# A static order planned in twelve passes forwards and backwards, and two squares moved to GpSimd, in a kernel of masked attention and a gated feed-forward network

## The chip, the cores and the metric

The kernel runs on one core of a Trainium2 chip. The metric is the device time of one execution in microseconds (us). PE is TensorE (the matrix unit), ACT is ScalarE, DVE is VectorE, POOL is GpSimd, and SP issues most DMAs.

## The reference

Attention over 8 batches, 8 heads, 576 positions and 64 channels: the first four heads see a local window of 32 positions, the other four every 32nd position. Its output is the input of a gated network of 4608 tokens with 512 channels and 1536 hidden ones. All is in 32-bit floats.

```python
scores = scale * np.matmul(q, k.transpose(0, 1, 3, 2))
mask_local = (rel >= 0) & (rel < stride)
mask_strided = (rel >= 0) & (pos[None, :] % stride == pos[:, None] % stride)
...
attn = attn / (np.sum(attn, axis=-1, keepdims=True) + 1e-09)
attn_out = np.matmul(attn, v)
...
rms = np.sqrt(np.mean(x * x, axis=-1, keepdims=True) + 1e-06)
xn = x / rms * rms_g
g = xn @ w_gate
silu = g * (1.0 / (1.0 + np.exp(-g)))
val = xn @ w_val
return (silu * val @ w_out).astype(np.float32)
```

## The kernel before

**Products.** The tokens are cut into 9 chunks of 512 and the hidden channels into 12 units of 128. A unit of a chunk is a `g` product, a `v` product and an `o` product, each in four groups of three matmuls of 128x512: both operands are split into a high and a low part, and the three matmuls are high by high, high by low and low by high (`xh`, `xl` for the input, `hh`, `hl` for the hidden values, `w` or `z` for the weights). `g` and `v` have one PSUM bank each. ACT takes the tanh of `g` (L835), DVE forms the gate from it and from `g` (L837, which frees the bank `g`) and multiplies by `v` (L849, which frees the bank `v`), ACT rounds the result to `hh` (L856), GpSimd forms the rest `hl` (L864), and one unit later the `o` product adds into four accumulators (L877). At the end of a chunk ACT or DVE copies each accumulator out (L884).

**Attention.** It comes in 96 units (batch, pair of heads, third of the rows), 12 for each batch of 576 tokens, a little ahead of the products that need them. Fifteen units run first; the others lie between the product groups. A unit is: scores on PE (L537, or L548 and L552 for the first 27), mask and maximum on DVE (L575, L577, L578), exp on ACT (L590), reciprocal of the sum on DVE (L595, L596), normalisation on GpSimd (L599), 32x32 transposes on DVE (L641; PE and ACT for the early units), the product with the values on PE (L678) and its evacuation to `raw` (L713). For each pair of heads after the 27th unit ACT rounds q and k (L444) and DVE subtracts to get their rests (L449). `raw` is squared and summed for the norm (L724 for chunk 0; L737, L742 and the matmul L747 later), scaled (L774, L778) and split into `xh` (L791) and `xl` (L806).

**Weights.** In the first 150 us each of 36 weight tiles is loaded and unpacked: L950, L957 and L970 on ACT, L961 and L963 on DVE, and a subtraction, L974, on GpSimd or DVE.

**What sets the order.** Nothing is emitted where it stands in the source. `op` records each step with its cost on each engine that could do it, and what it reads and writes. `Plan.order` then gives each step a due time, the length of the longest chain of costs from it to the end with its sign turned, and builds the schedule once, forwards: of the steps that can start, each engine takes the one that is due first, and of several engines the one that ends first. Steps marked `port` on DVE, and all of GpSimd, are never planned at the same time. The order of that schedule is the order in which each engine executes.

Of the kernel before, what the change touches and what calls it, by code (L numbers as in the profile page):

```python
# [94 lines left out]
NPB = 2  # L95
NTB = 3
SPU = 9
GRE = 'DVE'
RCE = 'ACT'
PP0 = 27  # L100
# [30 lines left out]
class Plan:  # L131
# [8 lines left out]
    def __init__(self):  # L140
        self.ops = []
        self.writer = {}
        self.readers = {}
        self.serial = False
        self.last_pe = None

# [24 lines left out]
        self.ops.append((ways, deps, bytes_, rel, lock, tab, chain))  # L171

    def order(self):
        ops, n = self.ops, len(self.ops)
        left = [len(o[1]) for o in ops]
        users = [[] for _ in range(n)]
        for i, o in enumerate(ops):
            for d in o[1]:
# [3 lines left out]
        for i in range(n - 1, -1, -1):  # L182
            ways, _, nb, _, _, _, chain = ops[i]
            eng = min(ways, key=lambda e: ways[e][0])
            own = ways[eng][0] + (DMT if nb else self.TAIL[eng])
            t = max([-due[u] + (0.0 if eng in ops[u][0] else self.LAT) for u in users[i]], default=0.0) + own
            if chain:
                t = chained = max(t, chained + ways[eng][0] * CHF)
            due[i] = -t
        end, on = [0.0] * n, [None] * n  # L190
        ready = [None] * n
        free, avail = {}, {}
# [27 lines left out]
        while len(out) < n:  # L220
            best = None
            for e, lst in avail.items():
                cand = []
                for i in lst:
                    s = start(i, e)
                    ways = ops[i][0]
                    if len(ways) > 1:
                        f = s + ways[e][0] - MARG
                        if any(x != e and start(i, x) + ways[x][0] < f for x in ways):
                            continue  # L230
                    cand.append((s, due[i], i))
# [12 lines left out]
            done = s + cost + self.TAIL[e]  # L244
            for b in lock:
                held[b] = (done, e)
            if pt:
                port = (done, e)
            for x in ways:
                avail[x].remove(i)  # L250
            free[e] = s + cost
            on[i] = e
            if nb:
                dma = max(dma, s) + nb / 380.0
                end[i] = dma + 2000.0
            else:
                end[i] = done
            out.append(fn)
            for u in users[i]:
                left[u] -= 1  # L260
                if not left[u]:
                    enter(u)
# [4 lines left out]
def attn_moe(ctx: ExitStack, tc: tile.TileContext, qT: bass.AP, kT: bass.AP, vl: bass.AP, vs: bass.AP,  # L267
# [151 lines left out]
    def split(o, at):  # L419
        first = 3 * o == FP  # L420

        def part(fn, src, key, more=()):
            ways = [("ACT", act(S), False), ("DVE", 375, True)] if not more else [("DVE", dve(S), True), ("Pool", pool(S), True)]
            if "g" not in ALT:
                ways = ways[:1]
            op(*ways[0][:2], at, fn, reads=[("xx", src)] + list(more), writes=[key], port=ways[0][2], also=ways[1:])
# [187 lines left out]
    def step_t(i):  # L614
# [35 lines left out]
        def trans():  # L650
# [1 line left out]
                nc.tensor.transpose(out=pp[:, x // nt, x % nt * m:(x % nt + 1) * m], in_=pv[:, x // nt, x % nt], identity=ident[:m, :m])  # L652
        op("PE", (PF if i < n_pro else 1) * 2 * nt * 0.85 * m + 30, at + PE_T, trans, reads=[pk, "ident"], writes=[TK, ("S", pn)] if i >= FP - 3 else [TK],
           lock=locks)
        op("ACT", act(2 * nt * m, True), at + 1500, lambda e: nc.scalar.copy(out=dv, in_=pp) if e == "ACT" else
           nc.vector.tensor_copy(out=dv, in_=pp), reads=[TK], writes=[tk], lock=locks, also=way("d", ("DVE", dve(2 * nt * m), False)))

    def step_o(units):

# [60 lines left out]
    def square(c, p, at):  # L720
        rt = raw[c % 2]
        dst, dk = (ssq, "ssq") if p % 2 == 0 else (srt, "srt")
        if c == 0:
            op("ACT", act(CH), at, lambda: nc.scalar.activation(out=dst, in_=rt[:, p], func=AF.Square),  # L724
               reads=[("raw", 0, p)], writes=[dk])

            def sums():
                for t in range(4):
# [53 lines left out]
    def convert(c, at, kcs=range(KC)):  # L782
        rt = raw[c % 2]
        for kc in kcs:
# [14 lines left out]
            def lo(e, kc=kc):  # L799
# [5 lines left out]
                else:  # L805
                    (nc.vector if e == "DVE" else nc.gpsimd).tensor_tensor(out=o, in0=i, in1=h, op=ALU.subtract)  # L806
            r = [("raw", c % 2, kc), "gt"]
            op("ACT", act(CH), at + kc, hi, reads=r, writes=[("xh", kc)] + [("spare", kc)] * (c == 0),
               also=way("j", ("DVE", 345, True)))
            op("DVE", dve(CH), at + kc, lo, reads=r + [("xh", kc)], writes=[("xl", kc)] + [("spare", 4 + kc)] * (c == 0), port=True,  # L810
               also=[("Pool", pool(CH), True)] if c else [])

# [122 lines left out]
    for x, key in enumerate(keys):  # L935
# [11 lines left out]
        def scale(e, hi32=hi32):  # L947
# [2 lines left out]
                nc.scalar.activation(out=h, in_=h, func=AF.Copy, scale=2.0 ** -112)  # L950
            else:
                nc.vector.tensor_scalar(out=h, in0=h, scalar1=2.0 ** -112, scalar2=None, op0=ALU.mult)
        op("ACT", 561, at, scale, writes=[("w", key)], rel=CV0 + CVP * x, also=way("a", ("DVE", 345, True)))

        def last3(e, lo32=lo32, top=top):
            if e == "ACT":
# [10 lines left out]
        def hi(e, key=key, z=z):  # L967
# [5 lines left out]
        op("ACT", act(512), at, hi, reads=[zk], writes=[("w", key), "worder"], also=way("c", ("DVE", 345, True)))  # L973
# [143 lines left out]
```

## Time and profile before

| | us |
|---|---|
| median of 3 runs | 1062.4 (1061.9 to 1063.38) |
| profiled execution | 1061.61 |
| its span, first to last instruction | 1059.8 |
| PE busy | 1028.4 |
| DVE busy | 704.6 |
| ACT busy | 545.1 |
| GpSimd busy | 284.5 |

A busy time counts stretches in which at least one instruction of the engine is under way. Matmuls are pipelined, so PE's stalls show best in the distance from one start to the next.

### The profile page before, as it was taken

How to read it: one execution, taken by the hardware profiler on the slowest of the kernel's cores; microseconds unless marked ns; L12 is line 12 of the kernel's file. 1: busy time of each engine (PE TensorE's matmuls, PEld its weight loads, DVE VectorE, ACT ScalarE, POOL GpSimd, SP SyncE). 2: the span in 40 equal slices, each digit the busy share in tenths (PEclk: the TensorE clock that was granted, in tenths of full speed). 3: DMA queues.
4: the chain of work that ended last, by engine and by line, in shares of the span. 5: the costliest groups of instructions: out<-in, count | busy, mean ns of one | idle time of the engine just before them, and what ended most of it. 6: DMA issues, size and time to landing. Idle time of an engine off the chain costs nothing.

```text
span 1059.8 us, 14841 instructions
## 1 busy us (share of the span) xinstructions
PE 1028.4 (97%) x5212; PEld 825.7 (78%) x5212; DVE 704.6 (66%) x1508; ACT 545.1 (51%) x1459; POOL 284.5 (27%) x263
## 2 busy tenths in 40 slices
PE   7989999999999999999999999999999999999998
PEld 5767667787788778887788788887888888878886
DVE  6899997688857877688757975888578631232111
ACT  6988855556455555555636554564545441132112
POOL 5213433232212321233122222222122322111111
PEclk9899999999999999999999999999999999999999
DMA  9854120211111111011111201111110010001001
GB/s 321 276 195 167 37 68 16 74 36 52 35 63 35 41 47 63 17 53 38 44 47 35 61 16 62 36 49 39 62 34 15 1 40 1 1 0 41 1 1 40
DMA packets 26715, 59.86 MB, mean 56 GB/s; under 512 B 2896, under 2 KB 7184, under 8 KB 26640
## 3 DMA queue, kind: packets, MB, share of 16 engines
q1 hardware_dynamic: 26320, 58.32, 16.9%
q8 instruction: 41, 0.67, 0.3%
q10 hardware_dynamic: 320, 0.59, 0.2%
q14 instruction: 34, 0.28, 0.1%
HBM read 49.46 MB, written 9.44 MB: 56 GB/s over the span
## 4 chain that ended last, share of the span: by engine, by line
PE 74%; DVE 13%; ACT 8%; issue 2%; DMA 2%; POOL 0%; ACTq 0%; POOLq 0%; SPq 0%; DVEq 0%
PE v L822 23%; PE g L822 23%; PE acc L877 21%; ACT qk L444 3%; PE pair L678 3%; DVE qk L449 2%; PE pair L537 2%; DVE pT L641 2%; DMA w<-in_wgv_dram 2%; DVE z L963 1%; DVE e L849 1%; ACT pp L590 1%; DVE w L961 1%; DVE e L837 1%; DVE w L974 1%
## 5 line engine op out<-in xcount | busy, mean ns | idle before, releaser
L864 POOL TENSOR_TENSOR hl<-e,hh 128x512 fp32r<-128x512 f32 x107 | 141.6, 1324 | 383.7 <-ACT hh L856 340.9
L822 PE MATMUL g<-xh,w 128*128 128x512 f32 x648 | 205.3, 398 | 5.9 <-DVE e L837 5.9
L822 PE MATMUL v<-xh,w 128*128 128x512 f32 x648 | 204.1, 396 | 1.7 <-DVE e L849 1.6
L837 DVE SCALAR_TENSOR_TENSOR e<-e,g 128x512 f32<-128x512 f32 x108 | 73.7, 683 | 192.0 <-ACT e L835 190.8
L877 PE MATMUL acc<-w,hh 128*128 128x512 f32 x648 | 200.8, 391 | 0.0
L599 POOL TENSOR_TENSOR pp<-pp,su 96x512 f32<-96x512 f32 (+3 forms) x87 | 85.7, 985 | 313.9 <-DVE su L596 256.7
L590 ACT ACTIVATE pp<-pp,mx 96x128 f32<-96x128 f32 (+2 forms) x296 | 114.0, 386 | 101.0 <-DVE mx L578 91.4
L641 DVE STREAM_TRANSPOSE pT<-pp 32x128 f32<-32x128 f32 (+1 forms) x489 | 141.5, 289 | 30.3 <-POOL pp L599 18.6
L835 ACT ACTIVATE e<-g 128x512 f32<-128x512 f32 x108 | 64.0, 593 | 161.4 <-PE g L822 148.1
L822 PEld LDWEIGHTS v<-xh,w 128*128 128x128 f32 x648 | 119.7, 189 | 29.4 <-DVE e L849 4.9
L822 PEld LDWEIGHTS g<-xh,w 128*128 128x128 f32 x648 | 116.8, 189 | 31.8 <-DVE e L837 8.5
L877 PEld LDWEIGHTS acc<-w,hh 128*128 128x128 f32 x648 | 121.0, 188 | 25.9 <-issue 0.2
L822 PE MATMUL g<-xl,w 128*128 128x512 f32 x324 | 127.0, 392 | 0.0
L822 PE MATMUL v<-xl,w 128*128 128x512 f32 x324 | 127.0, 392 | 0.0
L877 PE MATMUL acc<-w,hl 128*128 128x512 f32 x324 | 126.1, 389 | 0.0
L856 ACT CAST hh<-e 128x512 fp32r<-128x512 f32 x107 | 66.3, 620 | 112.4 <-PE acc L877 90.9
L444 ACT CAST qk<-xx 64x576 fp32r<-64x576 f32 x138 | 88.7, 671 | 8.7 <-PE pair L537 6.4
L849 DVE SCALAR_TENSOR_TENSOR e<-e,v 128x512 f32<-128x512 f32 x108 | 73.5, 681 | 16.2 <-PE v L822 10.4
L449 DVE TENSOR_TENSOR qk<-xx,qk 64x576 fp32r<-64x576 f32 x92 | 72.4, 787 | 2.9
L822 PEld LDWEIGHTS v<-xl,w 128*128 128x128 f32 x324 | 61.2, 189 | 13.4
L822 PEld LDWEIGHTS g<-xl,w 128*128 128x128 f32 x324 | 61.1, 189 | 13.2
L877 PEld LDWEIGHTS acc<-w,hl 128*128 128x128 f32 x324 | 60.8, 188 | 12.8
(166 smaller groups left out, 1490.9 us busy)
## 6 DMA issues: line engine op xcount, KB each, us to landing
w<-in_wgv_dram SPq DMA_DIRECT2D x18, 512.0 KB, 6.5
xx<-in_qT_dram SPq DMA_DIRECT2D x27, 288.0 KB, 2.9
xx<-in_kT_dram SPq DMA_DIRECT2D x25, 288.0 KB, 3.1
vt<-in_vl_dram SPq DMA_DIRECT2D x16, 384.0 KB, 5.3
vt<-in_vs_dram SPq DMA_DIRECT2D x16, 315.0 KB
w<-in_wo_dram SPq DMA_DIRECT2D x9, 512.0 KB, 6.4
out_dram<-ssq SPq DMA_DIRECT2D x17, 256.0 KB, 2.1
out_dram<-srt SPq DMA_DIRECT2D x17, 256.0 KB, 2.0
```

The source lines that it names most:

```text
L444: nc.scalar.copy(out=d, in_=s)
L449: (nc.gpsimd if eng == "Pool" else nc.vector).tensor_tensor(out=d, in0=s, in1=y.bitcast(F32), op=ALU.subtract)
L590: nc.scalar.activation(out=pv[:, h, x], in_=sp[h][:, x] if i < PM else pv[:, h, x], func=AF.Exp, scale=0.125 if i < PM else 1.0, bias=mx[: ...
L599: (nc.vector if e == "DVE" else nc.gpsimd).tensor_tensor(out=pv, in0=pv, in1=su.unsqueeze(3).broadcast_to([m, 2, nt, n]), op=ALU.mult)
L641: nc.vector.transpose(out=dst[32 * y:32 * y + 32, :, 32 * x:32 * x + 32], in_=src[32 * x:32 * x + 32, :, 32 * y:32 * y + 32])
L822: nc.tensor.matmul(out=bank[bk], lhsT=wt[:, w, sl], rhs=xhl[x, kc], start=(kc == 0 and i == 0), stop=(kc == KC - 1 and i == 2))
L835: op("ACT", act(CH, True), at + MO, lambda: nc.scalar.activation(out=e, in_=bank["g"], func=AF.Tanh, scale=0.5), reads=["g"], writes=[ek], ...
L837: op("DVE", dve(CH), at + MO, lambda: nc.vector.scalar_tensor_tensor(out=e, in0=e, scalar=1.0, in1=bank["g"], op0=ALU.add, op1=ALU.mult), ...
L849: op("DVE", dve(CH), at + MO, lambda: nc.vector.scalar_tensor_tensor(out=e, in0=e, scalar=0.5, in1=bank["v"], op0=ALU.mult, op1=ALU.mult), ...
L856: nc.scalar.copy(out=hh[h], in_=e)
L864: (nc.vector if n == "DVE" else nc.gpsimd).tensor_tensor(out=hl[h], in0=e, in1=hh[h].bitcast(F32), op=ALU.subtract)
L877: nc.tensor.matmul(out=acc[t], lhsT=x[h][:, sl], rhs=wt[:, w], start=(u == 0 and i == 0), stop=(u == NU - 1 and i == 2))
```

## The change

`Plan.order` now repeats. Each pass builds the schedule forwards as before (`forward`), keeping for each step its engine, start and end. `latest` then builds a schedule backwards from the end of that one, with the engines as chosen; the latest times at which the steps could start in it are the due times of the next pass. Of twelve passes the shortest schedule, by the planner's own costs, is emitted. The cost of the subtraction for q and k on DVE goes from 675 to 780 ns. Two of the four squares of chunk 0 (`SQP`) are a multiplication on GpSimd and no longer an activation on ACT. The lists `EVD`, `HID`, `WHD` and `XHD` would move other steps to DVE; they are empty. Some second engines are taken out of the source; the letters that allowed them (`"a"`, `"c"`, `"d"`) are not in `ALT = 'e'`.

```diff
+ROUNDS = 12
+BHOLD = 0.0
+SQP = (0, 1)
...
+        best = None
+        for k in range(ROUNDS):
+            took = self.forward(users, due)
+            length = max(t[3] for t in took)
+            self.lengths.append(length)
+            if best is None or length < best[0]:
+                best = (length, took)
+            due = self.latest(users, took, length)
+        return [ops[i][0][e][2] for i, e, _, _ in best[1]]
+
+    def latest(self, users, took, length):
+        ops, n = self.ops, len(self.ops)
+        on, long, prio = [None] * n, [0.0] * n, [0.0] * n
+        for i, e, s, d in took:
+            on[i], long[i], prio[i] = e, d - s, -d
+        left = [len(u) for u in users]
+        free, ready, start = {e: 0.0 for e in self.TAIL}, [0.0] * n, [0.0] * n
+        avail = {e: [i for i in range(n) if not left[i] and on[i] == e] for e in self.TAIL}
+        for _ in range(n):
+            best = None
+            for e, lst in avail.items():
+                if lst:
+                    t = max(free[e], min(ready[i] for i in lst)) + BHOLD
+                    k = min((prio[i], max(free[e], ready[i]), i) for i in lst if ready[i] <= t)
+                    if best is None or k[1] < best[0][1]:
+                        best = (k, e)
+            (_, s, i), e = best
+            avail[e].remove(i)
...
+            free[e] = max(s + ops[i][0][e][0], free[e])
+            start[i] = s + ops[i][0][e][0]
+            for d in ops[i][1]:
+                t = start[i] + (0.0 if on[d] == e and not ops[d][2] else self.LAT) + long[d] - ops[d][0][on[d]][0]
+                ready[d] = max(ready[d], t)
...
+        return [-x for x in start]
...
-            ways = [("ACT", act(S), False), ("DVE", 375, True)] if not more else [("DVE", dve(S), True), ("Pool", pool(S), True)]
+            ways = [("ACT", act(S), False), ("DVE", 375, True)] if not more else [("DVE", 780, True), ("Pool", pool(S), True)]
...
+            if p in SQP:
+                op("Pool", pool(CH), at, lambda: nc.gpsimd.tensor_tensor(out=dst, in0=rt[:, p], in1=rt[:, p], op=ALU.mult),
+                   reads=[("raw", 0, p)], writes=[dk])
```

The order differs on every engine. Over the whole program five weight subtractions (L974 before) and twelve subtractions for `xl` (L806 before) stand on GpSimd and no longer on DVE, and two evacuations on ACT and no longer on DVE; the broadcast of chunk 0's norm is evacuated by DVE instead of ACT. Lines of the source shift: L449 is L500 in the changed kernel, L595 is L646, L641 is L692, L837 is L893, L849 is L905, L864 is L920.

DVE, in the middle of a chunk, in the later part of a pair of heads, before: `pp` and `mx` belong to the mask and maximum, `su` to the sum, `e` to the gate, `qk` to the rests of q and k.

```order
L837 SCALAR_TENSOR_TENSOR e_96<-e_96,g_71 128x512
L449 TENSOR_TENSOR qk_1778<-xx0_79,qk_1778 64x576
L449 TENSOR_TENSOR qk_1778<-xx1_80,qk_1778 64x576
L449 TENSOR_TENSOR qk_1778<-xx0_79,qk_1778 64x576
L449 TENSOR_TENSOR qk_1778<-xx1_80,qk_1778 64x576
L641 STREAM_TRANSPOSE pT1_94<-pp1_92 32x4x32 x3
L595 TENSOR_SCALAR su0_105<-su0_105 108x2
L596 RECIPROCAL su0_105<-su0_105 108x2
L849 SCALAR_TENSOR_TENSOR e_96<-e_96,v_72 128x512
```

The changed kernel at the same place:

```order
L500 TENSOR_TENSOR qk_1700<-xx0_79,qk_1700 64x576
L893 SCALAR_TENSOR_TENSOR e_96<-e_96,g_71 128x512
L500 TENSOR_TENSOR qk_1700<-xx1_80,qk_1700 64x576
L500 TENSOR_TENSOR qk_1700<-xx0_79,qk_1700 64x576
L500 TENSOR_TENSOR qk_1700<-xx1_80,qk_1700 64x576
L905 SCALAR_TENSOR_TENSOR e_96<-e_96,v_72 128x512
L646 TENSOR_SCALAR su0_105<-su0_105 108x2
L647 RECIPROCAL su0_105<-su0_105 108x2
```

One subtraction now stands ahead of the first gate operation and three behind it, and the second gate operation follows them; the transposes stand ahead of all, and the sum's operations behind.

DVE, one pair of heads later in the same chunk, before:

```order
L449 TENSOR_TENSOR qk_1778<-xx0_79,qk_1778 64x576
L449 TENSOR_TENSOR qk_1778<-xx1_80,qk_1778 64x576
L449 TENSOR_TENSOR qk_1778<-xx0_79,qk_1778 64x576
L449 TENSOR_TENSOR qk_1778<-xx1_80,qk_1778 64x576
L837 SCALAR_TENSOR_TENSOR e_96<-e_96,g_71 128x512
L641 STREAM_TRANSPOSE pT1_94<-pp0_91 32x4x32 x3
L595 TENSOR_SCALAR su3_108<-su3_108 108x2
L596 RECIPROCAL su3_108<-su3_108 108x2
L571 SCALAR_TENSOR_TENSOR pp0_91<-pair_75,cb_68 96x2x128 x2
L577 SCALAR_TENSOR_TENSOR pp0_91<-pair_75,pp0_91 96x512
L578 TENSOR_REDUCE mx0_101<-pp0_91 96x4
L849 SCALAR_TENSOR_TENSOR e_96<-e_96,v_72 128x512
```

The changed kernel there:

```order
L692 STREAM_TRANSPOSE pT1_94<-pp0_91 32x4x32 x4
L626 SCALAR_TENSOR_TENSOR pp1_92<-pair_75,cb_68 108x2x108
L628 SCALAR_TENSOR_TENSOR pp1_92<-pair_75,pp1_92 108x2x108
L629 TENSOR_REDUCE mx3_104<-pp1_92 108x2
L500 TENSOR_TENSOR qk_1700<-xx0_79,qk_1700 64x576
L500 TENSOR_TENSOR qk_1700<-xx1_80,qk_1700 64x576
L500 TENSOR_TENSOR qk_1700<-xx0_79,qk_1700 64x576
L893 SCALAR_TENSOR_TENSOR e_96<-e_96,g_71 128x512
L500 TENSOR_TENSOR qk_1700<-xx1_80,qk_1700 64x576
L905 SCALAR_TENSOR_TENSOR e_96<-e_96,v_72 128x512
```

Four transposes, which stood between the maximum and the subtractions, now stand ahead of the scaling; three subtractions stand ahead of the first gate operation and one behind it; the second gate operation follows, and the other transposes, the sum and the scaling of the next scores stand behind it.

GpSimd, at the change from one chunk to the next (`pp` is a normalisation, `ssq` the sum of squares), before:

```order
L599 TENSOR_TENSOR pp1_92<-pp1_92,su1_106 96x512
L864 TENSOR_TENSOR hl0_761<-e_96,hh0_99 128x512
L742 TENSOR_TENSOR ssq_97<-ssq_97,srt_98 128x512
L864 TENSOR_TENSOR hl0_761<-e_96,hh0_99 128x512 x2
L599 TENSOR_TENSOR pp0_91<-pp0_91,su2_107 96x512
L864 TENSOR_TENSOR hl0_761<-e_96,hh0_99 128x512 x2
```

The changed kernel there:

```order
L650 TENSOR_TENSOR pp1_92<-pp1_92,su1_106 96x512
L797 TENSOR_TENSOR ssq_97<-ssq_97,srt_98 128x512
L920 TENSOR_TENSOR hl0_769<-e_96,hh0_99 128x512
L861 TENSOR_TENSOR xl2_594<-raw0_76,xh2_581 128x512
L861 TENSOR_TENSOR xl3_640<-raw0_76,xh3_625 128x512
L920 TENSOR_TENSOR hl0_769<-e_96,hh0_99 128x512
L650 TENSOR_TENSOR pp0_91<-pp0_91,su2_107 96x512
L920 TENSOR_TENSOR hl0_769<-e_96,hh0_99 128x512 x2
```

The last two subtractions for `xl` have come in between two `hl`. On PE the score matmuls and the `o` groups are moved by a few groups as well: before, runs of three or four `g` groups without a `v` group occur at two places of each chunk; in the changed order `g` and `v` groups take turns.

## Rows read from the trace of the kernel before

**Rows 1.** The page, part 1: busy us, share of the span, instructions.

```profile
PE 1028.4 (97%) x5212; PEld 825.7 (78%) x5212; DVE 704.6 (66%) x1508; ACT 545.1 (51%) x1459; POOL 284.5 (27%) x263
```

**Rows 2.** Windows by stage: length, busy us (instructions) by engine, PE clock, DMA.

```profile
12.00:62.00 50.00, 40.97 (x328) 33.44 (x327) 43.22 (x113) 46.36 (x151) 17.33 (x16) 0.86 0.93 331
62.00:140.00 78.00, 73.43 (x378) 55.27 (x377) 75.40 (x128) 65.86 (x155) 27.57 (x18) 0.98 0.27 96
...
461.40:574.10 112.70, 111.23 (x568) 90.03 (x569) 84.97 (x189) 61.20 (x170) 30.27 (x28) 1.00 0.15 44
```

**Rows 3.** Waits of PE: waiter and releaser, us in total, times, longest.

```profile
PE v L822 <- DVE e L849: 4.3, 10, 0.6
```

**Rows 4.** Timeline of PE, three places: start, us, instruction, count, idle before.

```profile
359.81 0.39 PE L822 MATMUL g<-xl,w 128*128 128x512 f32 x1
360.66 0.73 PE L822 MATMUL v<-xh,w 128*128 128x512 f32 x2 [0.47 <-DVE e L849]
...
377.18 0.28 PE L537 MATMUL pair<-qk 128*96 128x256 f32 x1
...
378.25 0.74 PE L822 MATMUL g<-xh,z 128*128 128x512 f32 x2
...
381.11 0.63 PE L537 MATMUL pair<-qk 128*96 128x256 f32 x4
382.30 0.72 PE L822 MATMUL v<-xh,z 128*128 128x512 f32 x2 [0.55 <-DVE e L849]
...
406.45 0.64 PE L537 MATMUL pair<-qk 128*96 128x256 f32 x4
406.92 0.62 PE L822 MATMUL g<-xh,w 128*128 128x512 f32 x2
407.39 0.39 PE L822 MATMUL g<-xl,w 128*128 128x512 f32 x1
...
413.52 0.39 PE L822 MATMUL v<-xl,w 128*128 128x512 f32 x1
414.35 0.73 PE L877 MATMUL acc<-z,hh 128*128 128x512 f32 x2 [0.44 <-ACT ssq L884]
```

**Rows 5.** Timeline of DVE at places 1 and 2.

```profile
354.94 0.68 DVE L837 SCALAR_TENSOR_TENSOR e<-e,g 128x512 f32<-128x512 f32 x1
355.65 3.11 DVE L449 TENSOR_TENSOR qk<-xx,qk 64x576 fp32r<-64x576 f32 x4
...
359.94 0.67 DVE L849 SCALAR_TENSOR_TENSOR e<-e,v 128x512 f32<-128x512 f32 x1
...
373.10 1.24 DVE L641 STREAM_TRANSPOSE pT<-pp 32x128 f32<-32x128 f32 x4
...
377.50 0.69 DVE L837 SCALAR_TENSOR_TENSOR e<-e,g 128x512 f32<-128x512 f32 x1
...
381.57 0.68 DVE L849 SCALAR_TENSOR_TENSOR e<-e,v 128x512 f32<-128x512 f32 x1
```

**Rows 6.** Timeline of ACT ahead of place 3.

```profile
405.76 1.13 ACT L791 CAST xh<-raw 128x512 fp32r<-128x512 f32 x2
...
413.73 0.57 ACT L884 COPY ssq<-acc 128x512 f32<-128x512 f32 x1
```

**Rows 7.** Groups by line and shape: busy us, mean ns of one, idle before.

```profile
L724 ACT ACTIVATE ssq<-raw 128x512 f32<-128x512 f32 x2 | 1.3, 634 | 0.0
...
L974 DVE TENSOR_TENSOR w<-z,w 128x512 fp32r<-128x512 f32 x22 | 15.5, 706 | 0.1
...
L974 POOL TENSOR_TENSOR w<-z,w 128x512 fp32r<-128x512 f32 x5 | 6.5, 1296 | 20.3 <-ACT w L970 13.6 <-DVE w L961 6.8
```

**Rows 8.** Timeline of GpSimd (POOL), one row.

```profile
116.67 3.14 POOL L599 TENSOR_TENSOR pp<-pp,su 96x512 f32<-96x512 f32 x1 [0.75 <-DVE su L596]
```

**Rows 9.** Timeline of PE at the last chunk's start.

```profile
953.18 0.39 PE L877 MATMUL acc<-z,hl 128*128 128x512 f32 x1
954.27 0.74 PE L822 MATMUL g<-xh,w 128*128 128x512 f32 x2 [0.71 <-DVE e L837]
```

More of the change, by code (lines that the diff above doesn't have):

```diff
@@ L97 @@
 SPU = 9
+ROUNDS = 12
+BHOLD = 0.0
+EVD = ()
+SQP = (0, 1)
+HID = ()
+WHD = ()
+XHD = ()
 GRE = 'DVE'
@@ L143, in __init__ @@
         self.readers = {}
+        self.lengths = []
         self.serial = False
@@ L174, in order @@
         ops, n = self.ops, len(self.ops)
-        left = [len(o[1]) for o in ops]
         users = [[] for _ in range(n)]
@@ L189, in order, with forward @@
             due[i] = -t
+        best = None
[25 more added lines that the diff above has]
+            avail[e].remove(i)
+            tail = long[i] - ops[i][0][e][0]
+            free[e] = max(s + ops[i][0][e][0], free[e])
[3 more added lines that the diff above has]
+                ready[d] = max(ready[d], t)
+                left[d] -= 1
+                if not left[d]:
+                    avail[on[d]].append(d)
+        return [-x for x in start]
+    def forward(self, users, due):
+        ops, n = self.ops, len(self.ops)
+        left = [len(o[1]) for o in ops]
         end, on = [0.0] * n, [None] * n
@@ L257, in order @@
                 end[i] = done
-            out.append(fn)
+            out.append((i, e, s, end[i]))
             for u in users[i]:
@@ L654, in step_t @@
            lock=locks)
-        op("ACT", act(2 * nt * m, True), at + 1500, lambda e: nc.scalar.copy(out=dv, in_=pp) if e == "ACT" else
-           nc.vector.tensor_copy(out=dv, in_=pp), reads=[TK], writes=[tk], lock=locks, also=way("d", ("DVE", dve(2 * nt * m), False)))
+        op(*(("DVE", dve(2 * nt * m)) if i in EVD else ("ACT", act(2 * nt * m, True))), at + 1500,
+           lambda e: nc.scalar.copy(out=dv, in_=pp) if e == "ACT" else nc.vector.tensor_copy(out=dv, in_=pp), reads=[TK], writes=[tk], lock=locks, also=[])
     def step_o(units):
@@ L723, in square @@
         if c == 0:
-            op("ACT", act(CH), at, lambda: nc.scalar.activation(out=dst, in_=rt[:, p], func=AF.Square),
-               reads=[("raw", 0, p)], writes=[dk])
+            if p in SQP:
+                op("Pool", pool(CH), at, lambda: nc.gpsimd.tensor_tensor(out=dst, in0=rt[:, p], in1=rt[:, p], op=ALU.mult),
+                   reads=[("raw", 0, p)], writes=[dk])
+            else:
+                op("ACT", act(CH), at, lambda: nc.scalar.activation(out=dst, in_=rt[:, p], func=AF.Square),
+                   reads=[("raw", 0, p)], writes=[dk])
             def sums():
@@ L807, in convert @@
             r = [("raw", c % 2, kc), "gt"]
-            op("ACT", act(CH), at + kc, hi, reads=r, writes=[("xh", kc)] + [("spare", kc)] * (c == 0),
-               also=way("j", ("DVE", 345, True)))
+            xd = c == 0 and kc in XHD
+            op(*(("DVE", 345) if xd else ("ACT", act(CH))), at + kc, hi, reads=r, writes=[("xh", kc)] + [("spare", kc)] * (c == 0),
+               port=xd, also=[] if xd else way("j", ("DVE", 345, True)))
             op("DVE", dve(CH), at + kc, lo, reads=r + [("xh", kc)], writes=[("xl", kc)] + [("spare", 4 + kc)] * (c == 0), port=True,
@@ L952, in scale @@
                 nc.vector.tensor_scalar(out=h, in0=h, scalar1=2.0 ** -112, scalar2=None, op0=ALU.mult)
-        op("ACT", 561, at, scale, writes=[("w", key)], rel=CV0 + CVP * x, also=way("a", ("DVE", 345, True)))
+        op(*(("DVE", 420) if x in HID else ("ACT", 561)), at, scale, writes=[("w", key)], rel=CV0 + CVP * x, port=x in HID, also=[])
         def last3(e, lo32=lo32, top=top):
@@ L972, in hi @@
                 nc.vector.tensor_copy(out=W[key][:, 0], in_=z)
-        op("ACT", act(512), at, hi, reads=[zk], writes=[("w", key), "worder"], also=way("c", ("DVE", 345, True)))
+        op(*(("DVE", 345) if x in WHD else ("ACT", act(512))), at, hi, reads=[zk], writes=[("w", key), "worder"], port=x in WHD, also=[])
         op("Pool", pool(512), at, lambda e, key=key, z=z: (nc.vector if e == "DVE" else nc.gpsimd).tensor_tensor(
```

## Prediction

> **What bounds the kernel now.** I began with the busy time by stage. PE has matmuls in flight for 1028.4 of 1059.8 us [rows 1], so only 31.4 us of the span are without one, and the windows say where they lie [rows 2]. From 12 to 62 us (the first fifteen attention units) PE misses 9.0 us, while ACT works 46.4 of 50. From 62 to 140 us (the first eight units of the matrix products, with the conversion of the weights beside them) PE misses 4.6, while DVE works 75.4 and ACT 65.9 of 78. After that PE is the bound: in one period of twelve units, 461 to 574 us, it misses 1.5 of 112.7 and DVE has a quarter of the time free. PE's work is the same before and after the change, so the change can only take away stalls, or make new ones.
>
> The list of waits tells which stalls the steady part has: PE's `v` product waits ten times, 4.3 us in all, for DVE's second gate operation, L849 [rows 3]. I call L837, which frees the `g` bank, A, and L849, which frees the `v` bank, B. The timeline of PE shows the stalls in one period. At place 1, the matmul at 359.81 us is followed only at 360.66, where a running stream has two starts in 0.47 us (406.92 to 407.39), so 0.23 for one and 0.68 for a group: 0.62 us lost. At place 2, four score matmuls begin at 377.18 and the next product at 378.25, 1.07 us where the same four take 0.47 elsewhere (406.45 to 406.92); the next scores begin at 381.11 and `v` follows at 382.30, 1.19 us. That is 0.60 and 0.72 us. At place 3, 413.52 to 414.35 us, another 0.60 [rows 4]. The first pair after a stall also takes 0.73 us where 0.62 is usual, 0.11 more. DVE's timeline shows the cause of the first two: at place 1 four subtractions of q and k (3.11 us, so 0.78 each), three transposes and two small operations stand between A and B, and B starts at 359.94, 4.3 us after A ended; at place 2 four transposes (1.24) stand ahead of the same four subtractions, and B starts 3.4 us after A ended, behind more transposes and the whole scaling of the next scores [rows 5]. At place 3 ACT is late: its evacuation of an accumulator starts at 413.73 [rows 6].
>
> **The change, part by part.** The options with empty lists, the dropped alternatives (their letters are not in `ALT`) and the costs that stand beside an empty list change no instruction; they cost nothing. What remains is the order, five weight subtractions and twelve of x that go from DVE to GpSimd, and two squares that go from ACT to GpSimd.
>
> Steady order. At place 1 one subtraction now stands ahead of A and three behind it, and B comes next; counted from the same point, B starts after 0.78 + 0.68 + 2.33 = 3.8 us, not after 0.68 + 4.3 = 5.0. That is 1.2 us earlier, against 0.62 lost. At place 2 the fourth subtraction, for which the scores wait, ends after 0.69 + 3.11 = 3.8 us, not after 1.24 + 3.11 = 4.35: 0.55 of the 0.60 lost, and PE comes to these scores three product groups later; B starts then too, 3.8 us after 373.10, not 8.5. PE's own order moves the same way: it had runs of three or four `g` groups without a `v` group, and now has `g` and `v` in turn. So I take places 1 and 2 as gone. What is late next are the transposes and scalings that now stand behind B, by up to 2.3 us; exp on ACT and the normalisation on GpSimd wait for them, with ACT working 61.2 of 112.7 us [rows 2]. Place 3 stays: between the start of the chunk and the evacuation ACT has the same casts and exps in both orders.
>
> The sum for five periods (their places repeat from 247 to 720 us): ten `v` waits, 4.3 us of idle, each with 0.16 more between the starts (0.62 lost for 0.47 idle), 5.9; five waits of the scores at 0.60, 3.0; fifteen restarts at 0.11, 1.6. In all 10.5. New stalls are not in any trace: at least none, at most one like place 3 (0.71) in each period, 3.6. I take half, 1.8: place 3 shows that the planner can leave one of that size in a period, and the two places that I laid out have more than they need. Term: 8.7 us less.
>
> Start. Two squares leave ACT, 2 x 0.634 us, and two casts of weights of the same size, taken at the same price, move behind its eighth `hh` cast [rows 7]: 2.5 us less on the engine that is full until 62 us and beyond. DVE loses five subtractions of 0.706, 3.5 us. The gain is what the fuller engine gains, ACT: 2.5; both together, 6.0, are the upper end. It lies inside the 13.6 us that PE misses there. Against it stands GpSimd: five subtractions at 1.296 and two multiplications, for which that is the nearest row, 9.1 us more. The squares stand in GpSimd's queue ahead of normalisations of later units, which wait if the evacuated tile is late; GpSimd works 17.3 of 50 us there, which covers it, and without that cover each costs its 1.3 us.
>
> GpSimd and DVE get in each other's way: a normalisation of 96x512 at 116.67 us took 3.14 us [rows 8], while DVE ran operations with two operands in SBUF, and a subtraction of 128x512 takes 1.3 [rows 7]. So the lower end is that each of the 9.1 us also holds DVE: 9.1 - 3.5 = 5.6 us more. The Trainium skill says this as a rule ("SBUF — State Buffer", section "SBUF: two separate sides": the port pair that DVE and GpSimd share is locked for a whole instruction, and the other fully blocks), and its page "Perfetto Trace Analysis", section "Optimizing Scalar/DVE Operations", adds that moving work between those two might not help. The 3.14 us agree with it in kind. By that rule alone the start would cost 5.6 us, where by ACT's list it gives 2.5. I take 2.5, since the planner keeps the operations that it marks as sharing a port apart, in both versions, and five moves spread over 78 us.
>
> End. Once, at 953.18 us, the first `g` of the last chunk comes 1.09 us after the matmul before it [rows 9]. The new order has sixteen product groups between the matmul of the row sums and this `g`, not fifteen: one more group, 0.68 us, of cover. Term: 0.7 less.
>
> The profiled execution took 1061.6 us, 0.8 less than the median of the three runs. 1061.6 - 8.7 - 2.5 - 0.7 = 1049.7, and with that 0.8, 1050.5 us.
>
> **Rivals.**
> (a) The stalls move instead of going. B is early, but exp, the normalisation or `hh` is late, and half of the 10.5 us comes back elsewhere. For it: DVE and ACT keep the same work, packed more tightly, and small deviations hit. Against: DVE is free a quarter of the time. With the start and end terms as above: 1054 to 1058 us.
> (b) GpSimd holds DVE at the start, as it may have at 116.67 us, with each of the seven moved steps. For it: the 3.14 us; DVE full until 140 us. Against: GpSimd idle two thirds of that stretch. 1061.6 - 8.7 + 5.6 - 0.7 + 0.8 = 1058.6 us.
> (c) Slower: the chunk boundary. At five boundaries the last two subtractions of x, and at three more the third, now run on GpSimd after ACT's casts, which end at 406.89 us (0.56 each, so the first is ready at 406.3) [rows 6], and the low half `hl` of the unit before stands behind them. At 1.3 us each they end at 408.9, and `hl`, of the same size, at 410.2. PE needs it in the third matmul of the eighth group after 406.92, at 406.92 + 7 x 0.68 + 0.45 = 412.1: 1.9 us of cover. If each of the three takes 3.14 us, `hl` comes at 415.7, and five boundaries stall 3.6 us each: 18, and 1050.5 + 18 = 1068.5 us. It decides (the gain of 11.9 is lost) when each stalls 2.4 us, that is when the three together take 8.2 us, not 3.9. Against it: in that stretch DVE runs A, B and scalings that read PSUM.
> (d) Nothing changes: PE is busy 97% and the planner's gain is one of its model alone; 1060.3 to 1064.5 us.
>
> **From cases to numbers.** Likeliest (places 1 and 2 go, place 3 stays): 0.55, 1044 to 1054 us by its own bounds (3.5 us more at the start, 1.8 without new stalls; 1.8 and 2 the other way). (a) 0.15, (b) 0.10, (d) 0.08, (c) 0.12. 0.2%, 2.1 us, is what a measurement of this kernel can just tell from no change. Faster: likeliest, (a), (b), 0.80; same 0.08; slower 0.12. The range goes from 1043 to 1059, which leaves out (c) and (d).
>
> **What would show it.** Right: in the new profile `v` hardly waits for B, no run of starts 0.85 us apart in the steady part, and a period of twelve units of 110.5 to 111 us where it was 112.7; place 3's 0.6 us wait on the evacuation is still there; the eighth unit is done 2 to 4 us earlier; PE misses some 22 us, not 31.4. Wrong: longer DVE operations or GpSimd ones of 2 to 3 us in the first 140 us (b), PE waiting for `hl` at the first products of a chunk (c), or new waits of PE on exp's successors or transposes (a).

## The result and the profile after

The changed kernel takes **1047.7 us** (median; 1045.85 to 1048.0), the kernel before 1062.81 beside it: ratio 0.9855, interval 0.9838 to 0.9872. The prediction was 1050.5 us, with a range of 1043 to 1059. The profiled execution took 1045.85 us; its span is 1044.1, 15.7 less than before.

Page part 1 of the changed kernel, to be held against [rows 1]:

```profile
PE 1020.0 (98%) x5212; PEld 822.9 (79%) x5212; DVE 703.4 (67%) x1490; ACT 540.5 (52%) x1458; POOL 315.8 (30%) x282
```

PE is without a matmul for 1044.1 - 1020.0 = 24.1 us, where it was 31.4 (the forecast was some 22). The other 8.4 us by which the span is shorter come off PE's busy time: 1.1 us in each steady period, 5.6 in five, and 3.1 ahead of the twelfth unit (169.4 to 166.4). GpSimd works 31 us more. The windows answer to [rows 2]:

```profile
12.00:62.00 50.00, 39.07 (x333) 31.28 (x333) 45.20 (x113) 45.15 (x157) 22.53 (x19) 0.93 0.91 332
62.00:140.00 78.00, 76.86 (x406) 59.29 (x406) 74.78 (x129) 67.07 (x157) 37.73 (x22) 1.00 0.27 95
407.40:517.70 110.30, 110.11 (x568) 90.16 (x567) 85.03 (x187) 60.72 (x173) 32.70 (x30) 1.00 0.14 45
```

A period of twelve units takes 110.3 us and no longer 112.7, and PE misses 0.2 us in it, not 1.5. The stretch from 62 to 140 us is also better filled (PE misses 1.1 us, not 4.6), that from 12 to 62 is not (10.9 for 9.0). The column of TensorE's granted clock rises as well: 0.93 and 1.00 in these two stretches, where it was 0.86 and 0.98. With 2.4 GHz as the full level and 1.2 GHz as the lower one, that is some 7 us at the lower level, where it was some 17. In the list of PE's waits, beside [rows 3], the row of the `v` product that waits for B (L905 now) is gone, and no wait for `hl` at the start of a chunk has come. Of the waits in this list two are shown; the first lies wholly ahead of 240 us, and from there to 930 us the second, place 3, is the only one:

```profile
PE g L878 <- DVE e L893: 4.8, 6, 1.5
...
PE acc L933 <- ACT ssq L940: 0.9, 5, 0.2
```

The timeline of PE, beside [rows 4]: the first `v` after B at place 1, the two groups of scores of place 2, then place 3, and the starts of two periods, 110.32 us apart.

```profile
353.86 0.39 PE L878 MATMUL g<-xl,w 128*128 128x512 f32 x1
354.08 0.62 PE L878 MATMUL v<-xh,w 128*128 128x512 f32 x2
...
371.15 0.64 PE L588 MATMUL pair<-qk 128*96 128x256 f32 x4
371.63 0.62 PE L878 MATMUL g<-xh,z 128*128 128x512 f32 x2
...
376.40 0.64 PE L588 MATMUL pair<-qk 128*96 128x256 f32 x4
376.88 0.62 PE L878 MATMUL v<-xh,z 128*128 128x512 f32 x2
...
405.26 0.39 PE L878 MATMUL v<-xl,w 128*128 128x512 f32 x1
405.85 0.74 PE L933 MATMUL acc<-z,hh 128*128 128x512 f32 x2 [0.20 <-ACT ssq L940]
...
407.36 0.63 PE L878 MATMUL g<-xh,w 128*128 128x512 f32 x2
...
517.68 0.62 PE L878 MATMUL g<-xh,w 128*128 128x512 f32 x2
```

At place 1 `v` follows 0.22 us after the matmul before it, 1.05 us after B's end. The scores of place 2 take 0.48 us to the next product, where they took 1.07 and 1.19. Place 3 has 0.59 us between the starts, where it had 0.83: it shrank by 0.24 and did not go. DVE's timeline at the two places, beside [rows 5], shows B (L905) 2.95 and 1.50 us after A (L893), where it was 5.00 and 4.07:

```profile
348.60 0.75 DVE L500 TENSOR_TENSOR qk<-xx,qk 64x576 fp32r<-64x576 f32 x1
349.39 0.69 DVE L893 SCALAR_TENSOR_TENSOR e<-e,g 128x512 f32<-128x512 f32 x1
349.99 2.32 DVE L500 TENSOR_TENSOR qk<-xx,qk 64x576 fp32r<-64x576 f32 x3
352.34 0.69 DVE L905 SCALAR_TENSOR_TENSOR e<-e,v 128x512 f32<-128x512 f32 x1
...
368.64 0.69 DVE L893 SCALAR_TENSOR_TENSOR e<-e,g 128x512 f32<-128x512 f32 x1
369.36 0.76 DVE L500 TENSOR_TENSOR qk<-xx,qk 64x576 fp32r<-64x576 f32 x1
370.14 0.69 DVE L905 SCALAR_TENSOR_TENSOR e<-e,v 128x512 f32<-128x512 f32 x1
```

The last chunk's start, beside [rows 9], has 0.42 us between the two starts, where it had 1.09:

```profile
938.10 0.39 PE L933 MATMUL acc<-z,hl 128*128 128x512 f32 x1
938.52 0.74 PE L878 MATMUL g<-xh,w 128*128 128x512 f32 x2
```

I count a unit as done 0.23 us after the start of its last `o` matmul. By stretches, before and after: to the twelfth unit 188.4 and 185.0 us; the five periods from there to unit 72 565.7 and 554.3; from 72 to 84 108.7 and 108.4; from 84 to the last 193.3 and 192.6. So the five periods gave 11.4 us, the start 3.4 and the rest 1.0.

### The profile page after: what moved, and what is told of

Same layout as the page of the kernel before. It is cut to its first block, busy times and chain, and to the rows that moved or that the text cites. A ratio compares the mean times of both kernels' runs of the same rounds, so it can differ in the third digit from the quotient of the medians.

```text
span 1044.1 us, 14859 instructions
## 1 busy us (share of the span) xinstructions
PE 1020.0 (98%) x5212; PEld 822.9 (79%) x5212; DVE 703.4 (67%) x1490; ACT 540.5 (52%) x1458; POOL 315.8 (30%) x282
## 4 chain that ended last, share of the span: by engine, by line
PE 79%; DVE 12%; ACT 5%; DMA 2%; issue 2%; ACTq 0%; POOLq 0%; POOL 0%; SPq 0%; DVEq 0%
PE acc L933 24%; PE g L878 24%; PE v L878 23%; PE pair L729 3%; PE pair L588 3%; ACT qk L495 2%; DVE z L1019 2%; DMA w<-in_wgv_dram 1%; DVE w L1017 1%; ACT pp L641 1%; DVE w L1030 1%; DVE e L893 1%; DVE qk L500 1%; DVE su L646 1%; PE g L802 1%
## 5 line engine op out<-in xcount | busy, mean ns | idle before, releaser
L920 POOL TENSOR_TENSOR hl<-e,hh 128x512 fp32r<-128x512 f32 x107 | 150.7, 1409 | 370.5 <-ACT hh L912 364.8
L893 DVE SCALAR_TENSOR_TENSOR e<-e,g 128x512 f32<-128x512 f32 x108 | 74.0, 685 | 187.0 <-ACT e L891 185.1
L641 ACT ACTIVATE pp<-pp,mx 96x128 f32<-96x128 f32 (+2 forms) x296 | 114.0, 387 | 108.7 <-DVE mx L629 102.0
L692 DVE STREAM_TRANSPOSE pT<-pp 32x128 f32<-32x128 f32 (+1 forms) x489 | 141.5, 289 | 26.7 <-POOL pp L650 14.8
L650 POOL TENSOR_TENSOR pp<-pp,su 96x512 f32<-96x512 f32 (+3 forms) x87 | 81.7, 939 | 256.2 <-DVE su L647 184.6
L905 DVE SCALAR_TENSOR_TENSOR e<-e,v 128x512 f32<-128x512 f32 x108 | 73.9, 684 | 18.6 <-PE v L878 12.4
L500 DVE TENSOR_TENSOR qk<-xx,qk 64x576 fp32r<-64x576 f32 x92 | 73.5, 799 | 2.7
L878 PEld LDWEIGHTS g<-xl,w 128*128 128x128 f32 x324 | 61.2, 189 | 13.2
```

Source lines behind the costliest of these rows:

```text
L500: (nc.gpsimd if eng == "Pool" else nc.vector).tensor_tensor(out=d, in0=s, in1=y.bitcast(F32), op=ALU.subtract)
L641: nc.scalar.activation(out=pv[:, h, x], in_=sp[h][:, x] if i < PM else pv[:, h, x], func=AF.Exp, scale=0.125 if i < PM else 1.0, bias=mx[: ...
L650: (nc.vector if e == "DVE" else nc.gpsimd).tensor_tensor(out=pv, in0=pv, in1=su.unsqueeze(3).broadcast_to([m, 2, nt, n]), op=ALU.mult)
L692: nc.vector.transpose(out=dst[32 * y:32 * y + 32, :, 32 * x:32 * x + 32], in_=src[32 * x:32 * x + 32, :, 32 * y:32 * y + 32])
L878: nc.tensor.matmul(out=bank[bk], lhsT=wt[:, w, sl], rhs=xhl[x, kc], start=(kc == 0 and i == 0), stop=(kc == KC - 1 and i == 2))
L893: op("DVE", dve(CH), at + MO, lambda: nc.vector.scalar_tensor_tensor(out=e, in0=e, scalar=1.0, in1=bank["g"], op0=ALU.add, op1=ALU.mult), ...
```

## The experiments

Twelve kernels ran. Ratios are to the kernel before on the same chip. Where nothing else is said, the kernel is the changed one with one edit.

| run | edit | median, us | ratio (interval) | period, us |
|---|---|---|---|---|
| before | | 1062.8 | 1 | 112.73 |
| changed | | 1047.7 | 0.9855 (0.9838 to 0.9872) | 110.32 |
| one_pass | one pass | 1068.48 | 1.0040 (1.0026 to 1.0054) | 113.56 |
| one_pass675 | one pass, old price | 1062.69 | 0.9983 (0.9971 to 0.9995) | 112.73 |
| two_pass | two passes | 1046.33 | 0.9829 (0.9813 to 0.9845) | 110.30 |
| sub675 | old price | 1046.46 | 0.9837 (0.9821 to 0.9853) | 110.33 |
| squares_act | four squares on ACT | 1049.05 | 0.9862 (0.9843 to 0.9881) | 110.32 |
| xl_dve | `xl` on DVE alone | 1047.61 | 0.9859 (0.9839 to 0.9879) | 110.33 |
| gate2_first | before, B moved | 1064.91 | 1.0010 (0.9998 to 1.0023) | 113.06 |
| gate2_hh | before, B and `hh` moved, long stretches | 1084.1 | 1.0195 (1.0172 to 1.0218) | 111.57 |
| gate2_hh_keep | before, B and `hh` moved | 1061.42 | 0.9989 (0.9975 to 1.0003) | 112.33 |
| gate2_hh_scores | as gate2_hh, scores moved too | 1087.89 | 1.0227 (1.0210 to 1.0243) | 111.84 |
| nt780 | no charge between products, thirteen passes | 1043.54 | 0.9819 (0.9802 to 0.9837) | 110.15 |
| nt675 | no charge between products, twelve passes, old price | 1046.72 | 0.9852 (0.9832 to 0.9872) | 110.13 |

The period is that of units 36 to 48 in the profiled execution.

**Which part of the change does it: passes, price or squares.**

```diff
-ROUNDS = 12
+ROUNDS = 1
```

> The changed kernel with one pass instead of twelve (the first pass has the old due times); the price of 780 for the subtraction and the two squares on GpSimd stay. If the repeated passes carry the gain of the steady part: the waits of the v product for the second gate operation are back (about ten, 4 us in all), a period of twelve units takes 112 to 113 us instead of 110.3, and the time is 1057 to 1062 us; the first eight units keep what the squares bring, 1.3 to 2.5 us. If the new price alone put the second gate operation early: 1047 to 1050 us and a period of 110.3.

1068.48 us, period 113.56, eleven waits of the `v` product: slower than the kernel before, and above the range that I gave. At this price the passes carry the whole gain, 1.0040 to 0.9855, that is 1.85% or 20 us, with the steps and prices otherwise the same. That it came out above 1062 left price and squares to be told apart:

```diff
-ROUNDS = 12
+ROUNDS = 1
...
-("DVE", 780, True), ("Pool", pool(S), True)]
+("DVE", dve(S), True), ("Pool", pool(S), True)]
```

> The changed kernel with one pass and with the old price of 675 for the subtraction; what is left of the change is the two squares on GpSimd. If the new price is what made the one-pass order slower than before, and the squares are worth 1.3 to 2.5 us: 1060 to 1062 us, a period of 112.7. If the squares hurt a one-pass order: 1066 to 1069, as with both.

1062.69 us, just above the first range, and period 112.73: the two squares alone are worth 0.17% (0.05 to 0.29%), 1.8 us, and the new price costs a one-pass order 0.57%, 6 us, though it is nearer to the measured 0.78 us.

```diff
-("DVE", 780, True), ("Pool", pool(S), True)]
+("DVE", dve(S), True), ("Pool", pool(S), True)]
```

> The changed kernel with the old price of 675 ns for the subtraction of q and k on DVE (its four instructions took 0.78 us each), twelve passes. If the passes alone remove the stalls: 1046.5 to 1049 us and no wait of the v product. If the passes need the right price, because an order packed for 675 is late by 0.4 us after four subtractions: stalls of 0.3 to 0.6 us behind each group of four, 1050 to 1055 us.

1046.46 us, at the lower edge of its first range, period 110.33, and no wait of the `v` product: with passes the price is not needed.

```diff
-ROUNDS = 12
+ROUNDS = 2
```

> The changed kernel with two passes instead of twelve, that is, one pass backwards. By the planner's own costs one pass is 1056.4 us, two are 1031.6, and the shortest of twelve is the fourth with 1027.2. If one set of latest times does nearly all: 1050 to 1054 us and a period near 110.3 to 111. If the stalls of the steady part need several passes: a period of 112 or more and 1058 to 1066 us.

1046.33 us, period 110.30: below what I gave it. One schedule built backwards does all that twelve passes do.

```diff
-SQP = (0, 1)
+SQP = ()
```

> The changed kernel with all four squares of chunk 0 on ACT again, twelve passes. If the squares are worth the ACT time that they free (two times 0.634, and at most two casts of weights as much again): 1049 to 1050.5 us, the eighth unit 1.3 to 2.5 us later than 142.4, the steady period unchanged at 110.3. If the whole gain of the start comes from the squares: the eighth unit is back near 147 and the time is 1052 to 1053.5. If GpSimd holds DVE there (the rival b of the prediction): 1045 to 1047, faster than the change.

1049.05 us; eighth unit done at 145.6 us, 3.2 later than in the change. The intervals of the two ratios overlap, so with passes the squares' worth is not told from nothing. The run excludes that they make the whole gain of the start, and shows no cost of the size of rival (b). The eighth unit comes later together with a lower clock: from 12 to 62 us the granted clock was 0.86, in the change 0.93.

**Is the late B the cause.** The change moves everything at once. So I took the kernel before and moved B alone:

```diff
+        for i, e, s, r in list(out):
+            if i in self.gate2 and s > 200000.0 and s - r > 1500.0:
+                at = out.index((i, e, s, r))
+                known = max(k for k, o in enumerate(out) if o[0] in ops[i][1])
+                to = next(k for k, o in enumerate(out) if k > known and o[1] == "DVE" and (o[2] >= r or k == at))
+                out.insert(to, out.pop(at))
```

> The kernel before, with its one pass and its order, except that the second gate operation is moved ahead on DVE at thirteen places after 200 us where the plan itself had it ready more than 1.5 us before its start: it goes in front of the subtractions, transposes or sums that stood ahead of it. PE's, ACT's and GpSimd's order stay. If the late second gate operation is the cause, as predicted: the ten waits of the v product go, 5.9 us, with their restarts, 1.1: 1055 to 1057 us; the wait of the scores at place 2 (0.60) stays. If PE's own order of g and v groups is the cause, or what is pushed behind becomes late: waits of the scores or of other products come instead, 1061 to 1064 us.

1064.91 us, no gain. The waits of the `v` product are gone, 4.3 us, and three others are new in the list, 4.8 us (scores are L544, B is L857, `hh` L864 and `hl` L872):

```profile
PE acc L885 <- POOL hl L872: 2.3, 5, 0.5
...
PE pair L544 <- DVE pp L584: 1.5, 5, 0.3
PE pair L544 <- ACT hh L864: 1.0, 5, 0.2
```

The timeline of PE at place 2 shows two of them:

```profile
491.48 0.28 PE L544 MATMUL pair<-qk 128*96 128x256 f32 x1
491.92 0.57 PE L544 MATMUL pair<-qk 128*96 128x256 f32 x3 [0.16 <-DVE qk L456]
...
495.89 0.71 PE L544 MATMUL pair<-qk 128*96 128x256 f32 x4 [0.33 <-DVE pp L584]
...
499.21 0.61 PE L885 MATMUL acc<-w,hh 128*128 128x512 f32 x2
500.28 0.50 PE L885 MATMUL acc<-w,hl 128*128 128x512 f32 x1 [0.45 <-POOL hl L872]
```

The wait for a subtraction is old ([rows 4] show it at 377.18); the other two came with the move. DVE's timeline there, from A to the end of the maximum:

```profile
491.81 0.69 DVE L844 SCALAR_TENSOR_TENSOR e<-e,g 128x512 f32<-128x512 f32 x1
...
493.50 0.69 DVE L857 SCALAR_TENSOR_TENSOR e<-e,v 128x512 f32<-128x512 f32 x1
...
494.38 0.73 DVE L578 SCALAR_TENSOR_TENSOR pp<-pair,cb 96x256 f32<-96x256 f32 x2
495.15 0.69 DVE L584 SCALAR_TENSOR_TENSOR pp<-pair,pp 96x512 f32<-96x512 f32 x1
495.87 0.68 DVE L585 TENSOR_REDUCE mx<-pp 96x4 f32<-96x512 f32 x1
```

And ACT's, where the exps (L597) wait for that maximum and the cast to `hh` (L864) stands behind them:

```profile
496.65 0.40 ACT L597 ACTIVATE pp<-pp,mx 96x128 f32<-96x128 f32 x1 [5.14 <-DVE mx L585]
...
498.11 0.19 ACT L597 ACTIVATION_READ_ACCUMULATOR pp<-pp,mx 96x1 f32 x1
498.20 0.60 ACT L864 CAST hh<-e 128x512 fp32r<-128x512 f32 x1
```

B ends early, at 494.2, but its cast starts 4.0 us later: it stands behind the exps in ACT's order, and ACT was idle for 5.14 us in front of them. So I moved the cast as well (`gate2_hh`), and then three score products of each period two groups later (`gate2_hh_scores`):

```diff
+                row = rows["ACT"]
+                at = next(k for k, o in enumerate(row) if o[0] == i + 1)
+                to = next(k for k, o in enumerate(row) if o[2] >= r + 900.0 or k == at)
+                row.insert(to, row.pop(at))
...
+                row = rows["PE"]
+                for j in [o[0] for o in row if o[0] in self.scores and r - 600.0 <= o[2] <= s + 400.0]:
+                    at = next(k for k, o in enumerate(row) if o[0] == j)
+                    row.insert(at + 2, row.pop(at))
```

> The kernel before with thirteen second gate operations ahead on DVE, as in the run before, and the cast to hh that follows each of them ahead on ACT as well, in front of the exps that stood ahead of it. PE's and GpSimd's order stay. The run before lost what it had won: 2.3 us because hl came late (its cast stood behind eight exp rows that waited for a later scaling) and 2.5 us in waits of the scores for the subtractions and for the scaling. If these are separate, the hl waits go and 2.3 us come back: 1062 to 1063 us, a period of 112.5 to 112.7. If ACT's exps become late instead: 1064 to 1067.

> As the run before this one, and on PE the three score products of each period that lie around a moved gate operation stand two product groups later. If the stalls of the steady part come from these three orders together (second gate operation, its cast, the scores), the hand-moved order gives most of the 10.5 us of the prediction: 1053 to 1057 us, a period of 110.6 to 111.4. If later scores only make the scalings and exps behind them late, the waits move once more: 1060 to 1066 us.

1084.1 and 1087.89 us. Both lost over 20 us ahead of 200 us, where nothing was moved: in the first the first unit was done at 84.7 us, where it is 69.2 in the kernel before, and the eighth at 172.8, where it is 147.1. Besides the moves these two kernels are written out in another way, each engine's steps in long stretches. So neither total says anything of the moves, and I ran the first again, with every engine's order the same and the steps interleaved as in the kernel before:

```diff
-            for e, row in rows.items():
-                while at[e] < len(row) and not need[row[at[e]][0]]:
...
+            heads = [(place[row[at[e]][0]], e) for e, row in rows.items() if at[e] < len(row) and not need[row[at[e]][0]]]
+            _, e = min(heads)
+            i = rows[e][at[e]][0]
```

> The same moves as in the run with the second gate operation and its cast to hh ahead (thirteen of each), and each engine's order the same as there; only the program text interleaves the engines as the kernel before does, where that run wrote each engine's steps in long stretches. If that writing cost the start (its first unit ended at 84.7 us, before at 69.2), and the moves are worth 1.17 us in a period: first unit near 69 to 71, period 111.6, 1056.5 to 1059.5 us. If the moves themselves cost the start: 1080 to 1086 us.

1061.42 us, not told from the kernel before, and above what I gave it: the period is 112.33, not 111.6. The writing was the cause of the lost start. The wait for `hl` is gone, but B and its cast together gain 0.4 us in a period, where the passes gain 2.4. What is left, in its list of waits (scores L561, subtraction L473, evacuation L911):

```profile
PE acc L904 <- ACT ssq L911: 2.2, 5, 0.4
...
PE pair L561 <- DVE pp L603: 1.6, 5, 0.3
...
PE pair L561 <- DVE qk L473: 1.2, 6, 0.4
PE pair L561 <- ACT pp L616: 0.9, 5, 0.2
```

That is 3.7 us in waits of the scores. Between the two kernels in long stretches, the later scores made the period 0.27 us longer: DVE then comes late to A, and in the list of `gate2_hh_scores` the waits of the `g` product for A went from 6.2 us in 6 to 11.2 in 11. This shift of the scores did not mend them, and no other was tried. With the start lost the total can't be held against my 1053 to 1057 us; the period can, and 111.84 is above the 110.6 to 111.4 that I gave.

**GpSimd's part.**

```diff
-               also=[("Pool", pool(CH), True)] if c else [])
+               also=[])
```

> The changed kernel with all subtractions for xl on DVE, as the plan could otherwise put twelve of them on GpSimd; twelve passes. If GpSimd's share neither holds DVE nor makes hl late (the forecast): 1046 to 1050 us, a period of 110.3. If the subtractions on GpSimd cost time at the chunk boundary (rival c in a milder form): 1042 to 1045. If the passes need GpSimd to take work from DVE: 1052 to 1058.

1047.61 us and the same period: the subtractions of x on GpSimd neither cost nor bring time that can be told here.

**A version beyond the change.** The planner adds 165 ns after each PE step also for a next one that writes the same bank. Without that charge there are two versions, `nt780` (its edit is shown) and `nt675` with twelve passes and the old price.

```diff
-ROUNDS = 12
+ROUNDS = 13
...
-                t = start[i] + (0.0 if on[d] == e and not ops[d][2] else self.LAT) + long[d] - ops[d][0][on[d]][0]
+                t = start[i] + ((0.0 if e != 'PE' else -self.TAIL[e]) if on[d] == e and not ops[d][2] else self.LAT) + long[d] - ops[d][0][on[d]][0]
...
-            ready[i] = {e: max([end[d] + (0.0 if on[d] == e and not ops[d][2] else self.LAT) for d in deps] + [rel]) for e in ways}
+            ready[i] = {e: max([end[d] + (-self.TAIL[e] * (e == 'PE') if on[d] == e and not ops[d][2] else self.LAT) for d in deps] + [rel]) for e in ways}
```

> The changed kernel with thirteen passes and one more price: between two groups of products that follow each other in the same bank the planner charged 165 ns on PE, where the trace starts matmul after matmul 0.23 us apart; now it charges nothing there. Its own length goes from 1027.2 to 1026.0. If the price kept PE's order from being packed better: 1043 to 1046.5 us. If it served as slack, and a tighter order is late more often: 1048 to 1054 us.

> The version without the 165 ns between products of one bank, with the old 675 for the subtraction and twelve passes: another order from the same price (its own length is 1026.6, in the run before 1026.0, in the change 1027.2). If the price is what gained 4 us in the run before: 1042 to 1045.5 us and a steady period of 110.1 to 110.2. If that order was a lucky one: 1046 to 1050 us, like the three other orders of several passes (1046.3, 1046.5, 1047.7).

1043.54 us with 780, the lowest median of the study: its interval lies just below that of the change, but overlaps those of `two_pass` and `sub675`. 1046.72 us with 675, above its first range and not told from `sub675`, which has the same price and the charge. From the twelfth unit to the last `nt780` and `nt675` take 853.1 and 852.9 us, the change takes 855.3 and `sub675` 854.5: 2.2 and 1.6 us come without the charge. The rest of the 4 us of `nt780` lies in the start, and that it comes from the charge is not shown. The twelfth unit is done at 183.4 us in `nt780` and at 187.1 in `nt675` (in the change at 185.0), and the granted clock from 12 to 62 us was 0.90 and 0.86.

## Why the prediction was right, and where it was not

**Steady order: right in its sum, 2.7 us too small, and with a reason that is only half of the cause.** The term was 8.7 us; the five periods gave 11.4. Places 1 and 2 went as forecast. The two sizes that missed are the allowance of 1.8 for new stalls (there were none) and place 3, which I kept and which shrank by 0.24 in each period, 1.2 in all: 8.7 + 1.8 + 1.2 = 11.7. The step that failed is a reason. I laid out that B comes 1.2 us earlier, and took what then stands behind B as covered, "with ACT working 61.2 of 112.7 us". The run with B alone shows that this cover isn't there: ACT was idle for 5.14 us just ahead of the exps and `hh` was late all the same, because it stood behind them. B early is not enough, and B and `hh` early gives 0.4 of 2.4 us. The passes, which bring the rest, also move subtractions, scalings, scores and products. Which of these moves carries how much is not settled: the one further move that was tried by hand, the later scores, did not gain.

**What makes the order good** is the backward pass, not the price and not the number of passes. Most of the loss stood in the plan itself. In the planner's own schedule (worked out by the program) the kernel before has a period of 111.38 us, and the chip took 112.73; one pass with the price of 780 has a period of 113.58 us, and the chip took 113.56; with twelve passes the plan has 109.21, and the chip took 110.33. Rival (d), a gain in the planner's model alone, falls. Against the kernel before the plan gains 2.2 us a period and the chip 2.4; against one pass at 780 some three quarters of the plan's gain, 3.2 of 4.4 us, came out on the chip.

**Start: in size not told.** 2.5 us were forecast, and the twelfth unit is done 3.4 us earlier (the eighth 142.4 for 147.1 us, a little beyond the 2 to 4 forecast). But profiled executions with the same start order differ as much: the kernel before, `gate2_first` and `gate2_hh_keep` have their twelfth unit at 188.4, 189.8 and 192.7. The time of the one-pass run with the old price gives the squares 0.5 to 3.1 us, which holds the 2.5, but in its profile the eighth unit is no earlier (147.6 us). And the forecast, which went by ACT's list, left out TensorE's clock. The change spends some 10 us less at the lower level ahead of 140 us; as an estimate from the two levels, that alone could make up to 5 us. The clock differs over the executions too: the mean granted clock of a whole execution was 0.995 to 0.997 in the four of the change and 0.990 to 0.995 in the four with the squares on ACT. How much of the 3.4 us is ACT's relief and how much the clock, and which of the two brings the other, is open.

**End: right.** 0.67 us less at the last chunk's first product, for 0.7.

**Rivals.** (a) did not come in the change, but it is just what each hand-moved order showed: the stalls moved. (b): its sign is there, its price is not. GpSimd's groups in the window from 62 to 140 us, first of the kernel before, then of the changed one and of `xl_dve`:

```profile
L864 POOL TENSOR_TENSOR hl<-e,hh 128x512 fp32r<-128x512 f32 x8 | 13.4, 1672 | 23.0 <-ACT hh L856 18.3 <-issue 4.7
```

```profile
L920 POOL TENSOR_TENSOR hl<-e,hh 128x512 fp32r<-128x512 f32 x8 | 22.1, 2758 | 27.2 <-ACT hh L912 26.2 <-ACT raw L764 1.0
```

```profile
L920 POOL TENSOR_TENSOR hl<-e,hh 128x512 fp32r<-128x512 f32 x8 | 15.7, 1966 | 44.4 <-ACT hh L912 39.0 <-DMA w<-in_wo_dram 5.5
```

And one of DVE's two unpacking groups (L963, L1019 in the change) in the window from 12 to 140 us, in the same three kernels:

```profile
L963 DVE SCALAR_TENSOR_TENSOR z<-w 128x512 uint32<-128x512 uint32 x27 | 21.0, 802 | 0.1
```

```profile
L1019 DVE SCALAR_TENSOR_TENSOR z<-w 128x512 uint32<-128x512 uint32 x27 | 19.1, 722 | 0.2
```

```profile
L1019 DVE SCALAR_TENSOR_TENSOR z<-w 128x512 uint32<-128x512 uint32 x27 | 22.2, 838 | 0.1
```

So in the change GpSimd's operations were stretched by 1.1 us, yet PE waits for none of them, and DVE's unpacking did not grow. Over the three kernels the two go against each other: where `hl` was shorter, this group took 802 and 838 ns, and where `hl` was long, 722 (the other group, L961, 800 and 799, then 759). The loss on DVE's side by which the start would have cost 5.6 us does not show in the change: there the loss was on GpSimd, and PE did not wait for it. The rule of the Trainium skill that the prediction quoted ("SBUF — State Buffer", section "SBUF: two separate sides"), that one of the two engines blocks while the other holds the shared ports, agrees with these rows in kind.

(c) PE waits for no `hl` at a chunk's start: at the five boundaries of the steady part the subtractions for `xl` on GpSimd took 1.3 us each, not 3.14. With `xl` on DVE the time is the same.

The price of 780, which I did not cost by itself, would have been worth a line: with one pass it alone costs 6 us. With twelve passes it makes no difference that can be told.

## What to carry to other kernels

When a static order loses time to stalls that stand in the planner's own schedule, plan once backwards and take the latest times as priorities: here one such pass gave all that twelve gave. Don't expect that from moving the one late instruction by hand; look first at what stands in order behind and ahead of its followers on their engines, since an engine that is half idle over a period can still hold the step that matters behind one that waits. A truer price for one instruction can make a one-pass order worse, so test prices and planner apart.

## What was not expected of the hardware and the program

The same steps in the same order on each engine took 1084.1 us when the program text ran through each engine in long stretches, and 1061.4 when it followed the plan's times. In the first, long waits stand at the start (DVE is idle for 7.25 us, up to 31.14 us, for a matmul), and TensorE's granted clock to the twelfth unit was 0.90, in the second 0.95; whether the waits bring the lower clock is not shown. Yet the first one's period is 0.76 us shorter, and 0.60 of that is place 3. PE's and ACT's timelines of `gate2_hh` there, and then PE's of `gate2_hh_keep`:

```profile
549.15 0.39 PE L849 MATMUL v<-xl,w 128*128 128x512 f32 x1
549.38 0.61 PE L905 MATMUL acc<-z,hh 128*128 128x512 f32 x2
...
550.26 0.59 ACT L912 COPY ssq<-acc 128x512 f32<-128x512 f32 x1 [0.80 <-PE acc L905]
```

```profile
528.91 0.39 PE L848 MATMUL v<-xl,w 128*128 128x512 f32 x1
529.74 0.74 PE L904 MATMUL acc<-z,hh 128*128 128x512 f32 x2 [0.45 <-ACT ssq L911]
```

In the one the evacuation waits for PE, in the other PE for the evacuation. So where a step stands in the text decided here who waits for whom, which the planner doesn't know. By what rule, and which waits differ at the start, is open.
